# Batch 0 of an attention and gated-MLP kernel: v requested before the second run of q and k, and that run's transposes moved behind the spread of the reciprocals

## The chip, the cores and the metric

One core of a Trainium2 chip. The metric is the device time of one execution in microseconds (us), the median over several executions. Every execution also leaves its span (first to last instruction, some 1.8 us shorter than the time).

## The reference

Sliding-window attention with a linear position bias, then a gated MLP. Cut to what matters:

```python
# q, k, v: (8 batches, 8 heads, 576 positions, 64); window 128
scores = q @ k.T / 8 + bias          # bias: -slope[head] * |i - j|
scores = where(0 <= i - j < 128, scores, -1e9)
attn = softmax(scores)
x = (attn @ v) as (4608 tokens, 512)
out = (gelu(x @ w_gate) * (x @ w_val)) @ w_out    # 512 -> 1536 -> 512
```

The kernel takes exp without subtracting the maximum, multiplies by exp of the bias (a mask that is 0 outside the window), sums, and multiplies the value products by the reciprocals of the sums.

## The kernel before

Everything is scheduled by hand: each engine runs its instructions in program order. Batch 0 is the head of the kernel: nothing can be overlapped with it except its own parts, so its transfers, transposes and exps are interleaved with care. Its positions are handled in two parts: part 0 is positions 0 to 319 (first run of q and k), part 1 is 320 to 575 (second run). All PSUM tiles come from one ring of eight banks, in program order.

The transfers, in order of issue:

```python
load_runs(0, 0, 0, 4)        # first run of q and k, heads 0..3
...
load_runs(0, 0, 4, 8)        # heads 4..7
load_runs(0, 1, 0, 8)        # second run of q and k
load_v(0, (0, 1, 2))         # v, the three tiles that part 0 needs
load_w(0, 256)               # gate and value weights, columns 0..255
load_w(256, 640)
...
```

The helpers that the change moves:

```python
def keep_busy(n): ...        # the next PSUM bank first takes n products of zeros (line 70)

def rest(cs):                # second run: transposes (line 151), two pairs of heads per bank
    for w in (0, 1):         # q, then k
        ps = bank().bitcast(BF16)
        for k, c in enumerate(cs):
            transpose_runs(0, 1, w, c, ps[:, 256 * k:256 * k + 256])
        untangle(act, 0, 1, w, slice(cs[0], cs[-1] + 1), ps)   # ONE copy on ACT (line 165)

def values_first(copies):    # part 0: value products (L358), copied out by ACT and DVE (L377),
    ...                      # spread of the reciprocals (L295), product of the two on DVE (L379)
```

And the head itself:

```python
scores(0, 0, (2, 3))         # scores, exps on ACT (L197), masks on DVE (L200)
scores2(0)
keep_busy(4)
rest((0, 1))
rest((2, 3))
keep_busy(3)
sums0(0)                     # 72 small products (L282), reciprocal on DVE (L286)
values_first((act, dve, act, dve))
scores(0, 1, (0, 1), None, masks)    # part 1: needs the copies of rest; eight exps
scores(0, 1, (2, 3), None, masks)
for f in range(4):
    gate_val(0, f, 0, 320, tails)    # gate and value products of part 0 (L392)
for args in masks:
    mask(*args)
made_last()                  # small memsets on DVE (L482 to L490)
for tail in tails[0:2]: tail()       # gelu on ACT (L398), gated product on DVE (L399)
sums0(1)                     # sums of part 1, second reciprocal
for tail in tails[2:4]: tail()
gate_val(0, 4, 0, 320)
spread4(0, 1, ...)           # second spread (L295)
```

The softmax here doesn't subtract the row's maximum and nothing guards it: scores larger than these inputs give would overflow.

Of the kernel before, what the change touches and what calls it, by code (L numbers as in the profile page):

```python
# [26 lines left out]
def kernel(  # L27
# [39 lines left out]
    def bank():  # L67
        ps = psum.tile([128, 512], FP32, name="ps")
        for _ in range(heat.pop()):
            nc.tensor.matmul(out=ps, lhsT=zeros[:, 0:128], rhs=zeros, start=True, stop=True)  # L70
        heat.append(0)
        return ps

    def keep_busy(n):
        heat[0] = n
# [20 lines left out]
    def load(t, src, b, js=range(5)):  # L96
        for j in js:
            lo = 64 if j == 0 else 0
            nc.gpsimd.dma_start(  # L99
                out=t[lo:128, j, :].rearrange("p (h d) -> p h d", h=H),  # L100
                in_=src[b][:, 128 * j - 64 + lo:128 * j + 64, :].rearrange("h p d -> p h d"))
# [10 lines left out]
    def runs(what, b, n):  # L112
        first, parts, r = RUNS[b][n]
        t, lo, p = (qs, ks)[what][b], 1536 * n, 0
        if (b, n) == (0, 1):

            t, lo = vb[1], 512 + 1024 * what
        elif b == 0:
            p = 64 * what
        return t.rearrange("p j x -> p (j x)")[p:p + parts, lo:lo + 512 * r].rearrange(  # L120
            "p (h x) -> p h x", h=H)

    def load_runs(b, n, h0, h1):
        first, parts, r = RUNS[b][n]
        for what, src in ((0, q), (1, k)):
            nc.gpsimd.dma_start(
                out=runs(what, b, n)[:, h0:h1, :],
                in_=src[b][h0:h1, first:first + parts * r, :].rearrange(
                    "h (p r) d -> p h (r d)", r=r))

    def load_v(b, js=range(5)):
        load(vb[b % 2], v, b, js)

    def load_w(lo, hi):
        for dst, src in ((wg, moe_w_gate), (wv, moe_w_val)):
            nc.gpsimd.dma_start(
                out=dst[:, :, lo:hi],
                in_=src[:, lo:hi].rearrange("(c p) f -> p c f", p=128))
# [5 lines left out]
    def transpose_runs(b, n, what, c, ps):  # L144

        first, parts, r = RUNS[b][n]
        src = runs(what, b, n)
        p = 64 * what if (b, n) == (0, 0) else 0
        for x in range(r):
            for i in (0, 1):  # L150
                nc.tensor.transpose(  # L151
                    out=ps[64 * i:64 * i + 64, parts * x:parts * x + parts],
                    in_=src[:, 2 * c + i, 64 * x:64 * x + 64],
                    identity=ident[p:p + parts, p:p + parts])

    def untangle(copy, b, n, what, c, ps):

        first, parts, r = RUNS[b][n]
        dst = by_pair((qT, kT)[what][b])[:, c, 64 + first:64 + first + parts * r]
        if isinstance(c, int):  # L160
            copy(out=dst.rearrange("p (x r) -> p x r", r=r),  # L161
                 in_=ps[:, 0:parts * r].rearrange("p (r x) -> p x r", r=r))
        else:
            n = c.stop - c.start
            copy(out=dst.rearrange("p c (x r) -> p c x r", r=r),
                 in_=ps[:, 0:n * parts * r].rearrange("p (c r x) -> p c x r", c=n, r=r))
# [22 lines left out]
    def score(b, c, i, j, qj, n, ps, col):  # L189
        nc.tensor.matmul(  # L190
            out=ps[:, col:col + 128 * n].rearrange("p (n t) -> p n t", n=n),
            lhsT=blocks(kT, b, i, c, j, 1).rearrange("p n t -> p (n t)"),
            rhs=blocks(qT, b, i, c, qj, n),
            start=True, stop=True)

    def exp(dst, src):
        nc.scalar.activation(out=dst, in_=src, func=AF.Exp, scale=0.125)  # L197

    def mask(dst, m):
        nc.vector.tensor_tensor(out=dst, in0=dst, in1=m, op=ALU.mult)  # L200

    def scores2(b, later=None):

        P = p2_pool.tile([128, 4, 2, 128], BF16, name="P2")
        probs2[b] = P
        ps = [bank(), bank()]
        for c in range(4):
            for i in (0, 1):
                score(b, c, i, 2, 2, 1, ps[i], 128 * c)
        for i in (0, 1):  # L210
            exp(P[:, :, i, :], ps[i].rearrange("p (c n) -> p c n", c=4))
        if later is None:
            for i in (0, 1):
                mask(P[:, :, i, :], emask[:, i:8:2, 0:128])
        else:
            later.append((P.rearrange("p c i n -> p (c i) n"), emask[:, :, 0:128]))

    def scores(b, s, cs, then=None, later=None):


        pss = []
        for c in cs:
            ps = [bank(), bank()]
            pss.append(ps)
            for j, qj, n, col in (((0, 0, 2, 0), (1, 1, 2, 256)),
                                  ((4, 4, 1, 0), (2, 3, 1, 128), (3, 3, 2, 256)))[s]:
                for i in (0, 1):
                    score(b, c, i, j, qj, n, ps[i], col)
        if then:
            then()  # L230
        for c, ps in zip(cs, pss):
            P = p_pool[s].tile([128, 2, 512], BF16, name="P")
            probs[b, s, c] = P
            for i in (0, 1):
                exp(P[:, i, :], ps[i])
            args = (P.rearrange("p i (n x) -> p i n x", n=2),
                    emask[:, 2 * c:2 * c + 2, :].unsqueeze(2).to_broadcast((128, 2, 2, 256)))
            if later is None:
                mask(*args)
            else:  # L240
                later.append(args)
# [46 lines left out]
    def spread4_banks(b, s):  # L288
        lo, w = PART[s][0], WIDE[s]

        pss = [bank() for _ in range(4)]
        n = (4, 2)[s]
        for k in range(n):
            for g, ps in enumerate(pss):
                nc.tensor.matmul(  # L295
                    out=ps[:, w * k:w * k + w],
                    lhsT=sel[32 * g:32 * g + 32, 2 * k:2 * k + 2, :].rearrange("p i m -> p (i m)"),
                    rhs=row(b)[32 * g:32 * g + 32, lo:lo + w], start=True, stop=True,
                    tile_position=(32 * g, 0))
        return pss  # L300
# [48 lines left out]
    def products(b, s, cs):  # L349
        lo, hi = PART[s]  # L350
        pss = []
        for c in cs:
            ps = bank()
            pss.append(ps)
            for j, a, e in PIECES[s]:
                for i in (0, 1):
                    h = 2 * c + i
                    nc.tensor.matmul(  # L358
                        out=ps[64 * i:64 * i + 64, a:e],
                        lhsT=vb[b % 2][:, j, 64 * h:64 * h + 64],  # L360
                        rhs=prob(b, s, c, i, j, e - a),
                        start=(j == 2 * s), stop=(j == 2 * s + 2), skip_group_check=True)
        return pss
# [8 lines left out]
    def values_first(copies):  # L372


        n, w = PART[0][1], WIDE[0]
        for c, ps in enumerate(products(0, 0, range(4))):
            copies[c](out=recip[0][:, c, 0:n], in_=ps[:, 0:n])  # L377
        for g, ps in enumerate(spread4_banks(0, 0)):
            nc.vector.tensor_tensor(  # L379
                out=xT[:, :, w * g:w * g + w], in0=recip[0][:, :, w * g:w * g + w],  # L380
                in1=ps[:, 0:4 * w].rearrange("p (c x) -> p c x", c=4), op=ALU.mult)
# [68 lines left out]
    for half, base, step, chan in ((0, 0, 1, -1), (1, -1, -1, 1)):  # L450
# [2 lines left out]
            out=t, in_=t, compare_op=ALU.is_ge, fill=1e9,  # L453
            base=base, pattern=[[step, 128]], channel_multiplier=chan)
    load_runs(0, 0, 4, 8)
    load_runs(0, 1, 0, 8)
    load_v(0, (0, 1, 2))
    load_w(0, 256)
    load_w(256, 640)
    load_v(0, (3, 4))  # L460
# [47 lines left out]
    def rest(cs):  # L508
        for w in (0, 1):
# [3 lines that stand above are left out]
            untangle(act, 0, 1, w, slice(cs[0], cs[-1] + 1), ps)  # L513
# [6 lines left out]
    keep_busy(2)  # L520
    scores(0, 0, (2, 3))
    scores2(0)
    keep_busy(4)
    rest((0, 1))
    rest((2, 3))
    keep_busy(3)
    sums0(0)
    masks, tails = [], []
    values_first((act, dve, act, dve))
    scores(0, 1, (0, 1), None, masks)  # L530
    scores(0, 1, (2, 3), None, masks)
    for f in range(4):
# [134 lines left out]
```

## Time and profile before

| | before |
|---|---|
| time, first 3 runs | 358.77 us (358.43 to 359.65) |
| span of the profiled execution | 356.0 us |
| last mask of part 0 ends | 13.02 us |
| sums of part 0 end | 14.47 us |
| eight exps of part 1 start | 17.15 us |
| second spread starts | 25.32 us |

The views are read as follows. The chain that ended last is followed back from the last instruction and gives, for each step, start, length and what ran. A timeline lists instructions in order of time, merged; what stands in brackets at a line's end is the idle time of that engine before it and what ended it. The lines of before are in the prediction below.

### The profile page before, as it was taken

What the parts mean: (1) busy time and instruction counts of PE and PEld (TensorE: products, weight loads), DVE (VectorE), ACT (ScalarE), POOL (GpSimd) and SP (SyncE); (2) the same over time, 40 slices, a digit from 0 to 9 for tenths busy, and PEclk for the clock granted to TensorE, in tenths of its full rate; (3) what the DMA queues carried; (4) which work ended last, traced back from release to release, by engine and by line L of the source; (5) the groups of instructions that cost most, each with busy time, mean ns of one, the idle gap of its engine ahead of it and who ended that gap; (6) DMA issues with size and microseconds to landing.
All of it is one profiled execution on the core that took longest, in us unless ns stands there. A gap on an engine that the chain in (4) does not pass through costs nothing.

```text
span 356.0 us, 7053 instructions
## 1 busy us (share of the span) xinstructions
PE 346.2 (97%) x2823; PEld 174.5 (49%) x2867; DVE 188.6 (53%) x327; ACT 185.8 (52%) x342; POOL 103.3 (29%) x137
## 2 busy tenths in 40 slices
PE   8899999999999999999999999999999999999995
PEld 3568545444454445445454545454444444444443
DVE  4785578344988646656456654755474404403320
ACT  6784495536877375633873297327832233313322
POOL 8853469600930193003900192004000000000000
PEclk9999999999999999999999999999999999999999
DMA  7999999999999299673996499759205020011002
GB/s 91 182 195 197 202 158 199 146 155 162 146 151 175 60 168 194 116 170 45 153 211 149 78 145 203 132 123 98 88 4 133 32 88 1 2 65 53 2 29 88
DMA packets 145632, 42.62 MB, mean 120 GB/s; under 512 B 131608, under 2 KB 138520, under 8 KB 145600
## 3 DMA queue, kind: packets, MB, share of 16 engines
q0 software_dynamic: 106368, 18.88, 69.4%
q1 hardware_dynamic: 36432, 17.31, 22.0%
q10 hardware_dynamic: 2800, 5.99, 7.7%
q8 instruction: 22, 0.36, 0.4%
q14 instruction: 10, 0.08, 0.1%
HBM read 43.65 MB, written 9.53 MB: 149 GB/s over the span
## 4 chain that ended last, share of the span: by engine, by line
PE 88%; DVE 5%; ACT 3%; issue 1%; DMA 1%; DVEq 0%; ACTq 0%; POOLq 0%
PE ps L392 51%; PE ps L415 23%; PE ps L358 5%; PE ps L190 4%; ACT P L197 3%; PE ps L315 2%; DVE P L200 1%; DVE r L321 1%; PE ps L151 1%; PE ps L70 1%; DMA qs<-in_q_dram 1%; PE ps L429 1%; DVE kT L161 1%; PE ps L295 1%; DVE hT L399 0%
## 5 line engine op out<-in xcount | busy, mean ns | idle before, releaser
L399 DVE TENSOR_TENSOR hT<-ps,gelu 128x512 bf16<-128x512 f32 (+2 forms) x115 | 74.3, 653 | 106.4 <-PE ps L392 92.5
L398 ACT ACTIVATE gelu<-ps 128x512 bf16<-128x512 f32 (+2 forms) x115 | 65.1, 571 | 115.5 <-PE ps L392 113.7
L392 PE MATMUL ps<-xT,wv 128*128 128x512 bf16 (+2 forms) x453 | 111.4, 366 | 0.6
L392 PE MATMUL ps<-xT,wg 128*128 128x512 bf16 (+2 forms) x444 | 110.4, 366 | 0.9
L415 PE MATMUL ps<-wo,hT 128*128 128x512 bf16 x402 | 94.6, 380 | 0.8
L197 ACT ACTIVATE P<-ps 128x512 bf16<-128x512 f32 x144 | 73.0, 632 | 8.1 <-PE ps L190 8.0
L392 PEld LDWEIGHTS <-wv 128*128 128x128 bf16 x460 | 44.7, 98 | 48.7
L392 PEld LDWEIGHTS <-wg 128*128 128x128 bf16 x460 | 43.2, 98 | 47.3 <-issue 0.5
L200 DVE TENSOR_TENSOR P<-P,emask 128x1024 bf16<-128x1024 bf16 (+1 forms) x79 | 49.1, 641 | 31.5 <-ACT P L197 31.0
L415 PEld LDWEIGHTS <-hT 128*128 128x128 bf16 x420 | 38.9, 98 | 47.7 <-issue 3.6
L99 POOL DMA_DIRECT2D vb<-in_v_dram x40 | 33.9, 886 | 10.6 <-DMA ks<-in_k_dram 4.3
L420 ACT COPY osb<-ps 128x512 f32<-128x512 f32 x31 | 18.7, 602 | 31.2 <-PE ps L415 30.4
L620 POOL COPY mark<-hT 1x2 bf16<-1x2 bf16 x4 | 0.7, 176 | 98.6 <-DVE hT L399 98.6
L321 DVE RECIPROCAL r<-ps 128x320 f32<-128x320 f32 (+1 forms) x14 | 26.8, 1935 | 1.3 <-PE ps L315 1.3
L99 POOL DMA_DIRECT2D qs<-in_q_dram x30 | 25.2, 857 | 7.2 <-DMA wo<-in_moe_w_out_dram 5.1
L368 DVE TENSOR_TENSOR xT<-ps,rb 128x256 bf16<-128x256 f32 (+1 forms) x60 | 22.9, 445 | 7.2 <-DMA rb<-rd 4.7
L99 POOL DMA_DIRECT2D ks<-in_k_dram x30 | 25.4, 884 | 1.2 <-DMA vb<-in_v_dram 0.7
L190 PE MATMUL ps<-qT,kT 64*128 64x256 bf16 (+1 forms) x384 | 22.1, 244 | 1.6 <-DVE kT L161 0.7
L190 PEld LDWEIGHTS <-kT 64*128 64x128 bf16 x384 | 13.4, 94 | 13.5 <-issue 9.9
L358 PE MATMUL ps<-P,vb 128*64 128x128 bf16 (+2 forms) x384 | 18.3, 244 | 0.1
L358 PEld LDWEIGHTS <-vb 128*64 128x64 bf16 x384 | 14.6, 110 | 5.4 <-issue 4.8
L398 ACT ACT_TABLE_LOAD x7 | 9.0, 1283 | 0.4 <-PE ps L392 0.3
(72 smaller groups left out, 115.2 us busy)
## 6 DMA issues: line engine op xcount, KB each, us to landing
out_dram<-osb SPq DMA_DIRECT2D x35, 256.0 KB, 3.3
rb<-rd ACTq DMA_DIRECT2D x10, 576.0 KB, 7.5
vb<-in_v_dram POOLq DMA_DIRECT2D x32, 128.0 KB, 6.8
qs<-in_q_dram POOLq DMA_DIRECT2D x24, 128.0 KB, 5.9
ks<-in_k_dram POOLq DMA_DIRECT2D x24, 128.0 KB, 6.3
wo<-in_moe_w_out_dram POOLq DMA_DIRECT2D x2, 768.0 KB, 17.5
wg<-in_moe_w_gate_dram POOLq DMA_DIRECT2D x2, 384.0 KB, 9.9
wv<-in_moe_w_val_dram POOLq DMA_DIRECT2D x2, 384.0 KB, 11.0
```

The costliest lines, as they stand in the source:

```text
L99: nc.gpsimd.dma_start(out=t[lo:128, j, :].rearrange("p (h d) -> p h d", h=H), in_=src[b][:, 128 * j - 64 + lo:128 * j + 64, :].rearrange(" ...
L190: nc.tensor.matmul(out=ps[:, col:col + 128 * n].rearrange("p (n t) -> p n t", n=n), lhsT=blocks(kT, b, i, c, j, 1).rearrange("p n t -> p ( ...
L197: nc.scalar.activation(out=dst, in_=src, func=AF.Exp, scale=0.125)
L200: nc.vector.tensor_tensor(out=dst, in0=dst, in1=m, op=ALU.mult)
L321: nc.vector.reciprocal(row(b)[:, lo:hi], ps[:, 0:hi - lo])
L358: nc.tensor.matmul(out=ps[64 * i:64 * i + 64, a:e], lhsT=vb[b % 2][:, j, 64 * h:64 * h + 64], rhs=prob(b, s, c, i, j, e - a), start=(j == ...
L368: nc.vector.tensor_tensor(out=xT[:, c, b * S + lo:b * S + hi], in0=ps[:, 0:hi - lo], in1=recip[b][:, c, lo:hi], op=ALU.mult)
L392: nc.tensor.matmul(out=ps[:, 0:hi - lo], lhsT=w[:, c, 128 * f:128 * (f + 1)], rhs=xT[:, c, t0 + lo:t0 + hi], start=(c == 0), stop=(c == 3))
L398: nc.scalar.activation(out=gl[:, 0:hi - lo], in_=pg[:, 0:hi - lo], func=AF.Gelu)
L399: nc.vector.tensor_tensor(out=hid[g][:, f, lo:hi], in0=pv[:, 0:hi - lo], in1=gl[:, 0:hi - lo], op=ALU.mult)
L415: nc.tensor.matmul(out=po, lhsT=hid[g][:, f, 128 * t:128 * (t + 1)], rhs=wo[:, f, :], start=(f == 0), stop=(f == NF - 1))
L420: (nc.vector.tensor_copy if g < 2 and t < 2 else nc.scalar.copy)(out=osb, in_=po)
```

## The change

The intent, by its own words: v arrives early enough for the value products, the sums follow the masks at once instead of behind transposes and products of zeros, and the second run's transposes move behind the spread, where their data (now later) has landed.

```diff
     load_runs(0, 0, 4, 8)
+    load_v(0, (0, 1, 2))
     load_runs(0, 1, 0, 8)
-    load_v(0, (0, 1, 2))
     load_w(0, 256)
@@
     scores2(0)
-    keep_busy(4)
-    rest((0, 1))
-    rest((2, 3))
-    keep_busy(3)
+    keep_busy(5)
     sums0(0)
     masks, tails = [], []
     values_first((act, dve, act, dve))
+    rest((0, 1))
+    rest((2, 3))
     scores(0, 1, (0, 1), None, masks)
```

## The prediction

> **What bounds the kernel now.** I read the page first, then the chain that ended last in order of time, then the timelines of ACT, DVE and TensorE from 8 to 28 us, then the landing times of the first transfers. From the page, the chain by engine and line:
>
> ```profile
> PE 88%; DVE 5%; ACT 3%; issue 1%; DMA 1%; DVEq 0%; ACTq 0%; POOLq 0%
> PE   8899999999999999999999999999999999999995
> ```
>
> TensorE is 9 tenths busy or more from the third slice on, and the waits of TensorE show no single one over 0.4 us after the start. So behind about 27 us the kernel is a rigid train of matmuls: whatever the first 27 us gain or lose arrives at the end nearly undiminished. The change touches only that head. The chain there (start us, length us, what):
>
> ```profile
> 10.51 0.97 PE ps L70 x4
> 11.48 1.17 PE ps L151 x32
> ...
> 13.02 0.38 PE ps L70
> 13.40 0.74 PE ps L282 x25
> ...
> 14.47 1.26 PE ps L358 x24
> 15.73 1.06 PE ps L295 x32
> 16.79 0.37 PE ps L190 x6
> 17.16 4.02 ACT P L197 x8
> ...
> 21.21 0.69 DVE P L200
> ...
> 23.66 0.74 DVE hT L399 x2
> 24.40 0.88 DVE r L286
> ...
> 25.32 0.73 PE ps L295 x16
> ```
>
> In words: products of zeros (L70), transposes of the second run (L151), zeros again, the sums of batch 0 (L282), the value products (L358), the spread of the reciprocals (L295), the first scores of the second part (L190). Then the chain leaves TensorE: eight exps on ACT in a row (17.16 to 21.18), the last mask on DVE, small memsets on DVE, two gated products, the second reciprocal, and at 25.32 back to TensorE. Between 18.70 and 25.1 TensorE is busy with the first gate and value matmuls, but they do not set the time of the second spread: the exps do. So the number to follow is the start of those eight exps, 17.15 us. ACT and DVE around it (start, length, line, the idle time before in brackets):
>
> ```profile
> 9.52 3.04 ACT L197 ACTIVATE P<-ps 128x512 bf16<-128x512 f32 x6 [0.34 <-PE ps L190]
> 12.40 0.65 ACT L165 COPY qT<-ps 128x512 bf16<-128x512 bf16 x1
> ...
> 13.82 0.70 ACT L165 COPY kT<-ps 128x512 bf16<-128x512 bf16 x1
> ...
> 17.15 4.03 ACT L197 ACTIVATE P<-ps 128x512 bf16<-128x512 f32 x8 [1.20 <-PE ps L190]
> ```
> ```profile
> 9.75 3.27 DVE L200 TENSOR_TENSOR P<-P,emask 128x1024 bf16<-128x1024 bf16 x6
> 14.51 0.66 DVE L286 RECIPROCAL r<-ps 128x80 f32<-128x80 f32 x1 [1.48 <-PE ps L282]
> ```
>
> The masks that the sums need end at 9.75 + 3.27 = 13.02, but the sums end at 14.47: DVE idles 1.48 us before the reciprocal. That is the slack the change goes for. The four copies of the second run's transposes (one each 0.47 us or so, 12.40 to 14.52) lie in ACT time that nobody needs. That is what the change gives away.
>
> **What the Trainium skill says.** "Perfetto Trace Analysis", Tensor Engine Instruction, says ACT and DVE are strict FIFO and only TensorE reorders, and there only weight loads. The trace agrees: ACT runs its copies and exps in program order. So in the changed kernel the eight exps cannot pass the four copies now put right ahead of them. "ScalarE: Activation LUTs", What ACT_TABLE_LOAD costs, gives 186 ns + 0.833 ns per element for an ACTIVATE with immediates and 93 ns of overlap, an estimate of 520 ns pitch at 512 elements; the trace has 4.03 us for eight, 0.50 us each, and I use that. "DMA: Bandwidth & Descriptors", Two DMAs through the same engine are not ordered, says descriptors of one queue start in order, though they need not finish so. The trace agrees in effect: landings follow the order of issue. "TensorE: Matmul & The Clock Gate", Part 1, says an idle window of about 3.4 us halves the clock. The granted clock was 1.00 in every stretch of the first 40 us here, among them 9 to 10 us, where TensorE was busy 0.50 us of 1.00.
>
> **The change part by part.**
>
> 1. The transfers. v (three tiles) moves ahead of the second run of q and k; sizes and count stay. Before, from issue plus landing: q 5.16 + 5.1 = 10.3, k 6.05 + 5.7 = 11.8, v 12.2, 14.0 and 14.7 us.
>
> ```profile
> vb<-in_k_dram POOLq DMA_DIRECT2D x1, 256.0 KB, 5.7
> ```
> ```profile
> vb<-in_v_dram POOLq DMA_DIRECT2D x2, 128.0 KB, 6.3
> 14.74 0.77 PEld L358 LDWEIGHTS <-vb 128*64 128x64 bf16 x20 [0.20 <-DMA vb<-in_v_dram]
> ```
>
> The last v (issued 8.49, landing 6.2 later) was even waited for, 0.20 us. In the changed order v takes the issue slots from 5.16 on. The three v tiles came within 2.9 us of the landing before them, and the first half's last k landed at 4.56 + 3.4 = 8.0, so my estimate is v complete at about 11 to 11.5, well before 13.2 where it is needed. The same bytes then end with k at about 14.7. Everything behind (weights) keeps its place.
>
> 2. The front of the path. Removed ahead of the sums: 32 transposes (1.17 us) and 2 of the 7 products of zeros. Five of these at about 0.24 us (four took 0.97) end at 10.51 + 1.2 = 11.7. From there the sums follow the masks. Those of the first 64 matmuls wait for all but the last mask. After 13.02 remain the last 8 of 72; at 1.07 us for 72 that is 0.12, plus some 0.05 of signalling: sums end at 13.2 instead of 14.47, a gain of 1.27. The value products take 1.06 (1.26 less the 0.20 wait): 14.26. The reciprocal (13.25 + 0.66 = 13.9) is in time for the spread, 1.06 as before: spread ends at 15.33 instead of 16.79, a gain of 1.46. None of the banks used is late: they come from exps that ended by 12.56 and from copies.
>
> 3. The back of the path. Now 32 transposes follow the spread, 15.33 to 16.5. The first eight fill a bank after about 0.33 (before, a group of ten took from 7.83 to 8.15), so ACT starts copying at 15.66. It has been free since the copies of the value products (c0 and c2, done near 14.6). Four copies at the measured pitch of 0.48 (12.40, 12.86, 13.34, 13.82) keep ACT until 15.66 + 1.92 = 17.58. The scores need the second copy (about 16.9), so their first bank is full near 17.3; the exps wait for ACT and not for scores. Exps start at 17.58 against 17.15: a loss of 0.43. In terms of the sum: minus 1.46 on the front, plus 0.33 + 1.92 for transposes and copies, minus the 0.37 of scores that is now covered by the copies = +0.42, about +0.4.
>
> 4. What hangs on it. Exps, last mask, memsets, two gated products and the reciprocal follow without slack on ACT and DVE (4.02 + 0.69 + about 1.8 + 0.74 + 0.88), so the second spread moves from 25.32 to about 25.75. The gate matmuls in between: their banks come from the exps of the first pair (done near 18.6), so they start at about 18.5, like before (18.70), and are done in time. xT for them is ready at about 17.1 rather than 18.55, a gain with no taker. The 0.48 us of zeros saved is TensorE time that turns into idle. After 26 us the same train, 0.4 us later: 358.77 + 0.4 = 359.2 us.
>
> **The rivals.** First: the front's gain reaches the end, because the copies overlap with the scores and the first exps need only the first two. Then 358.77 − 1.4 = about 357.4. For it speaks DVE's idle 1.48 us; against it the program order, which has all four copies ahead of the first exp, and ACT in FIFO order. Second: the moved q and k land late, or wait behind v, and TensorE stands at the transposes. If k landed at 16.5 instead of 14.7, the path would lose about another 1 us: 360.2. Against: the sum of the bytes ahead of it is unchanged, 14.7 stays some 0.9 ahead of need. Third: without zeros in the gaps (my estimates: 0.5 us before 17, 0.4 before 17.9, 0.3 before 13.0) the clock drops for one window; half of 3.4 us lost at most, about 361. Against: no gap is near that window, and as sparse a stretch kept full clock. Fourth: the 0.4 is absorbed, because the second spread has other slack; then 358.8. Against: the chain passes through it.
>
> **Range and chances.** My step lengths are good to some 0.1 us each, with a dozen of them, so ±0.4 on the shift; the three runs before spread from 358.43 to 359.65 themselves. Predicted 359.2, eight in ten between 358.2 and 360.2. Two per cent is 7.2 us, more than everything that lies between 10.5 us and 17.2 us could give or take: within 2% has 0.98; slower by more, through a clock or transfer accident, 0.015; faster 0.005.
>
> **What would show each step.** Right, if in the changed kernel: the sums end at 13.1 to 13.4 and DVE's wait for them shrinks to near 0.2; no wait on v; spread ends near 15.3; ACT's four copies stand at 15.6 to 17.6 directly ahead of the eight exps with no idle time between; the exps start at 17.4 to 17.8; the second spread is at 25.6 to 25.9; behind it the matmul train is the same, shifted. Wrong, if the exps start before 17.15 (then a gain), if TensorE waits on a transfer at the transposes, if the granted clock falls below 1.00 between 12 and 20 us, or if the second spread no longer follows the exps.

## The result

| | runs | median | range |
|---|---|---|---|
| changed | 4 | 358.78 us | 358.52 to 359.07 |
| before | 4 | 358.60 us | 358.37 to 359.65 |

The ratio is 1.000, 95% interval 0.9978 to 1.0021. Ratios here are the mean time of one kernel's fast runs over that of the other's of the same rounds, so not quite the ratio of the medians quoted. The time is the same within 2%, inside the predicted range. No change at all would have been inside it too; whether the small shift of 0.4 us was right needs the profile and more runs.

The chain of the changed kernel in the same stretch, start, length and what:

```profile
10.03 3.20 DVE P L200 x6
...
13.28 0.32 PE ps L282 x6
13.60 1.11 PE ps L358 x24
14.71 1.14 PE ps L295 x32
...
16.64 0.59 ACT kT L165
17.23 0.49 ACT qT L165
17.72 0.49 ACT kT L165
18.21 3.94 ACT P L197 x8
...
25.36 0.88 DVE r L286
...
26.28 0.73 PE ps L295 x16
```

The chain now runs through the masks of DVE, then the sums, and then, where before six scores led from the spread to the exps, through the copies of the transposes on ACT. ACT's timeline has the same without a gap:

```profile
16.16 0.59 ACT L165 COPY qT<-ps 128x512 bf16<-128x512 bf16 x1 [1.23 <-PE ps L151]
...
18.07 4.07 ACT L197 ACTIVATE P<-ps 128x512 bf16<-128x512 f32 x8
```

DVE's masks and first reciprocal:

```profile
9.95 3.27 DVE L200 TENSOR_TENSOR P<-P,emask 128x1024 bf16<-128x1024 bf16 x6
13.63 0.66 DVE L286 RECIPROCAL r<-ps 128x80 f32<-128x80 f32 x1 [0.41 <-PE ps L282]
```

DVE's idle time before the first reciprocal fell from 1.48 to 0.41 us: the front did gain. Yet the exps start at 18.07 instead of 17.15 and the second spread at 26.28 instead of 25.32, 0.96 us later. Far behind it the same group of gate products, before and after:

```profile
64.01 1.03 PE L392 MATMUL ps<-xT,wg 128*128 128x512 bf16 x4
```
```profile
64.97 1.03 PE L392 MATMUL ps<-xT,wg 128*128 128x512 bf16 x4
```

The span is 356.9 instead of 356.0 us. In these two executions nothing of the shift is absorbed.

Not all of the 0.92 us is the change's. The masks of part 0 already start at 9.95 instead of 9.75, and the reason lies ahead of everything that was changed. TensorE's first transposes, before and after:

```profile
4.53 0.50 PE L151 MATMUL ps<-ident,qs 64*64 64x64 bf16 x20 [0.27 <-DMA qs<-in_q_dram]
```
```profile
4.45 0.74 PE L151 MATMUL ps<-ident,qs 64*64 64x64 bf16 x20
```

The same twenty transposes took 0.50 us in one execution and 0.74 in the other, because TensorE came up to full speed somewhat later: the trace's clock record first grants it at 4.01 us before and at 5.23 after. Measured from the start of the masks, the exps stand 8.12 us later in the changed kernel and 7.40 in the one before: 0.72 us is the change's own.

### The profile page after: what moved, and what is told of

Same layout as the page of the kernel before. It is cut to its first block, busy times and chain, and to the rows that moved or that the text cites. A ratio compares the mean times of both kernels' runs of the same rounds, so it can differ in the third digit from the quotient of the medians.

```text
span 356.9 us, 7091 instructions
## 1 busy us (share of the span) xinstructions
PE 348.8 (98%) x2865; PEld 174.5 (49%) x2865; DVE 189.0 (53%) x327; ACT 185.8 (52%) x342; POOL 103.3 (29%) x137
## 3 DMA queue, kind: packets, MB, share of 16 engines
q0 software_dynamic: 106368, 18.88, 69.5%
## 4 chain that ended last, share of the span: by engine, by line
PE 90%; DVE 6%; ACT 2%; DMA 1%; issue 1%; ACTq 0%; DVEq 0%; POOLq 0%
PE ps L392 51%; PE ps L415 25%; PE ps L358 5%; PE ps L190 4%; DVE P L200 2%; PE ps L315 2%; ACT P L197 1%; DVE r L321 1%; DMA qs<-in_q_dram 1%; PE ps L429 1%; PE ps L151 1%; DVE kT L161 1%; PE ps L295 1%; PE ps L70 1%; DVE hT L399 0%
## 5 line engine op out<-in xcount | busy, mean ns | idle before, releaser
L392 PE MATMUL ps<-xT,wg 128*128 128x512 bf16 (+2 forms) x460 | 112.3, 366 | 0.1
L415 PE MATMUL ps<-wo,hT 128*128 128x512 bf16 x420 | 95.8, 380 | 0.0
L99 POOL DMA_DIRECT2D vb<-in_v_dram x40 | 34.0, 889 | 13.1 <-DMA ks<-in_k_dram 5.5
L358 PEld LDWEIGHTS <-vb 128*64 128x64 bf16 x384 | 14.7, 110 | 5.2 <-issue 4.8
```

The source lines that it names most:

```text
L99: nc.gpsimd.dma_start(out=t[lo:128, j, :].rearrange("p (h d) -> p h d", h=H), in_=src[b][:, 128 * j - 64 + lo:128 * j + 64, :].rearrange(" ...
L358: nc.tensor.matmul(out=ps[64 * i:64 * i + 64, a:e], lhsT=vb[b % 2][:, j, 64 * h:64 * h + 64], rhs=prob(b, s, c, i, j, e - a), start=(j == ...
L392: nc.tensor.matmul(out=ps[:, 0:hi - lo], lhsT=w[:, c, 128 * f:128 * (f + 1)], rhs=xT[:, c, t0 + lo:t0 + hi], start=(c == 0), stop=(c == 3))
L415: nc.tensor.matmul(out=po, lhsT=hid[g][:, f, 128 * t:128 * (t + 1)], rhs=wo[:, f, :], start=(f == 0), stop=(f == NF - 1))
```

## The experiments

Twelve runs of nine kernels were made, in four batches, each batch on one chip with its own runs of the kernel before. What the times have in common, first: in every batch some executions, also of the kernel before, are longer than the others by mostly 2 us or a little more. Of the 44 runs of before in the four batches, 33 lie between 357.67 and 358.94 us and 11 between 359.90 and 360.49. Five profiles fell into long executions, all by chance, and all show why. One of them (the last version, second time), first TensorE by time, then the same kernel's row for 4 to 9 us (length, busy time of PE, PEld, DVE, ACT and POOL, then granted clock, DMA share, GB/s):

```profile
9.13 1.04 PE L70 MATMUL ps<-zeros 128*128 128x512 bf16 x2
```
```profile
4.00:9.00 5.00, 4.58 (x53) 2.05 (x53) 2.31 (x6) 2.72 (x9) 5.00 (x7) 1.00 1.09 133
```

Two products of zeros take 1.04 us at 9.13 us; in the profile of before, at 4.96 us, the same two take 0.61. The row prints a granted clock of 1.00 all the same, but this is the view's doing: the trace's clock record has no entry before full speed is first granted, and the view counts a stretch without an entry as full. The first entry stands at 9.24 to 10.62 us in these five profiles and at 3.94 to 5.23 us in the others (6.13 in that of experiment 3), and the masks of part 0 start at 11.9 to 12.4 us instead of 9.8 to 10.1 (10.4 in experiment 3). I call them late starts. For the runs without a profile this is inferred from the time alone. Where it matters, I give medians without the runs that are longer by this gap and say so.

**1. The changed kernel again.**

> The changed kernel as it is, again, in five rounds. Both profiles so far differ by 0.92 us at the start of the eight exps, by 0.96 at the second spread and by 0.9 in the span, while the medians of the timed runs differ by only 0.2. Theory A (the shift of the head reaches the end, part of it is chance between two executions): 0.4 to 0.9 us slower than before, exps at 17.9 to 18.2 us. Theory B (it is absorbed later): within 0.2 us of before although the exps stand late again.

Six runs: five of 358.58 to 358.77 and one of 361.37. Ratio to before 1.0021 (0.9992 to 1.0051). Without the long run of either kernel (one of 6, one of 11) the medians are 358.69 and 358.1: 0.6 us slower. The profile has the masks at 9.85, the exps at 17.96, 8.11 us behind them, and the second spread at 26.18. This agrees with theory A, and not with B. The interval of the ratio includes 1, so the time alone does not prove a loss; the two profiles, equal to 0.01 us from masks to exps, show that the shift of the exps repeats. In this second profile v was complete only at 13.1 us and k at 15.8, so the transfers were nearly late, though no instruction waits for them.

**2. The order alone: transposes moved, transfers as before.**

```diff
     load_runs(0, 0, 4, 8)
-    load_v(0, (0, 1, 2))
     load_runs(0, 1, 0, 8)
+    load_v(0, (0, 1, 2))
```

> The new order of the matmuls, but v again behind the second run of q and k. If v must be early for the new order, the value products wait for the last v at about 14.7 us instead of starting at 13.5, the exps start near 19.1 and the span is about 1.0 us over the changed kernel's. If v's place did not matter, the exps stay at 18.1.

Ratio 1.0061 (1.0038 to 1.0084), six runs from 359.81 to 361.68. The three shorter ones have a median of 359.98, 1.3 us above the changed kernel's 358.69. The profile fell into a late start, where v had landed when it was wanted (exps at 20.42), so it was taken again:

> The new order with v behind, again, for a profile: the first profile fell into an execution in which TensorE ran its first products at half speed until 9.4 us, so that v had landed when it was wanted. In an execution that is fast from 4.5 us on I expect a wait of about 1.0 us on v within the value products and the exps near 19.1; in a slow one, no wait and the exps near 20.4.

```profile
14.19 1.40 PE L358 MATMUL ps<-P,vb 128*64 128x256 bf16 x22 [0.27 <-DMA vb<-in_v_dram]
```
```profile
14.59 0.77 PEld L358 LDWEIGHTS <-vb 128*64 128x64 bf16 x20 [0.30 <-DMA vb<-in_v_dram]
18.95 4.07 ACT L197 ACTIVATE P<-ps 128x512 bf16<-128x512 f32 x8
```

This execution ran at full speed from about 5.3 us. The value products wait for v and the exps start at 18.95, as expected (near 19.1), 0.9 us later than in the changed kernel. So the new order needs v early.

**3. The transfers alone: the order as before, v ahead.**

```diff
     load_runs(0, 0, 4, 8)
-    load_runs(0, 1, 0, 8)
     load_v(0, (0, 1, 2))
+    load_runs(0, 1, 0, 8)
```

> The order of the matmuls of before, with v requested ahead of the second run of q and k. If the two parts of the change need each other, the transposes of k stand ahead of the sums and wait for k, which then lands at 15.2 to 15.7 us instead of 11.8; 24 transposes, the zeros, sums, products, spread and scores follow, so the exps start near 20.9 and the time rises by 3.5 to 4 us. If TensorE's clock also drops in the wait of nearly 4 us (the rival of the prediction on the clock), matmuls behind it take twice as long for a while and the time rises by 5 us or more. If v's place alone brought something, the time would not rise.

Ratio 1.0103 (1.0077 to 1.0130), runs 361.39 to 362.59. The transposes wait for q and for k, and then the clock falls; TensorE by time, and then two stretches of time, columns as above (granted clock is the third figure from the end):

```profile
13.93 0.41 PE L151 MATMUL ps<-ident,vb 128*64 128x128 bf16 x8 [1.79 <-DMA vb<-in_q_dram]
15.42 0.86 PE L151 MATMUL ps<-ident,vb 128*64 128x128 bf16 x24 [1.08 <-DMA vb<-in_k_dram]
```
```profile
16.00:18.00 2.00, 1.78 (x49) 0.90 (x47) 0.00 (x0) 1.44 (x3) 1.14 (x2) 0.59 1.33 203
18.00:20.00 2.00, 2.00 (x66) 1.83 (x58) 0.66 (x1) 0.28 (x1) 0.74 (x1) 0.55 1.38 198
```

Both halves of the change are losses by themselves, and they belong together. By the ratio the rise is 3.7 us, by the medians (362.3 against 358.08 for before without its two long runs) 4.2, where I expected 3.5 to 4 from the waits and 5 or more with a fall of the clock. The clock did fall: the profile has the exps at 21.96, 4.8 us later than before, of which 0.7 is a later start of the masks. So the fall cost less than I had set for it. The trace's record has the clock at one half from 16.37 to 19.79 us; the two rows above are means over that. It also gives the prediction's third rival its due: such a fall exists, and here it came after more idle time than the changed kernel has. In the 3.41 us before 16.37 TensorE was busy 1.36 us; in the changed kernel's stretch of that length with the gaps behind the spread, 15.47 to 18.88 us, it was busy 2.54 and the clock stayed full.

**4. Half of the copies back under the masks ("split").** The helpers `load_runs` and `rest` take one more argument for this, which of q and k to handle; that part of the diff is left out.

```diff
     load_runs(0, 0, 4, 8)
+    load_runs(0, 1, 0, 8, (0,))     # q of the second run
     load_v(0, (0, 1, 2))
-    load_runs(0, 1, 0, 8)
+    load_runs(0, 1, 0, 8, (1,))     # k of the second run
@@
-    keep_busy(5)
+    keep_busy(2)
+    rest((0, 1), (0,))              # transposes of q
+    rest((2, 3), (0,))
+    keep_busy(2)
     sums0(0)
@@
     values_first((act, dve, act, dve))
-    rest((0, 1))
-    rest((2, 3))
+    rest((0, 1), (1,))              # transposes of k
+    rest((2, 3), (1,))
```

> The changed kernel with q's half of the second run back in the wait for the masks: q's transfer stands before v, k's behind, q's transposes ahead of the sums, k's behind the spread; two of the four ACT copies lie again before 13.6 us. If the four copies ahead of the exps are what costs, the exps start 0.9 to 1.0 us earlier than in the changed kernel (17.0 to 17.3), and the span is 0.7 to 1.0 lower. If late transposes or the transfers cost, and not the copies, little of it comes back: the exps at 17.7 or later.

```profile
12.60 1.14 ACT L165 COPY qT<-ps 128x512 bf16<-128x512 bf16 x2
...
16.16 1.07 ACT L165 COPY kT<-ps 128x512 bf16<-128x512 bf16 x2 [1.23 <-PE ps L151]
17.23 4.03 ACT L197 ACTIVATE P<-ps 128x512 bf16<-128x512 f32 x8
```

The first copy behind the spread starts at 16.16 us, exactly as in the changed kernel; only two of the four copies have gone from there, and the exps start 0.84 us earlier. The time: ratio to before 1.0010 (0.9976 to 1.0044), with two long runs of six; the other four have a median of 357.86, 0.8 us below the changed kernel's 358.69 of the same batch. This is the test of the main step: the copies on ACT ahead of the exps are what holds the exps: two copies at the measured pitch of 0.48 us are 0.96, the exps came 0.84 us earlier, and the time without long runs fell by 0.8. The transposes do not hold them: both copies and the exps follow each other on ACT without a gap. (One of the two long runs, 361.49, is longer by 3.6 us, which is more than a late start explains.)

**5. The memsets early, in the changed kernel.**

```diff
+    made_last()
     for args in masks:
         mask(*args)
     masks.clear()
-    made_last()
```

> The changed kernel with the small memsets of DVE moved ahead of the second part's masks, into the 1.7 us in which DVE then waits for the exps. If the chain exps, last mask, memsets, gated products, reciprocal sets the second spread, this takes the 1.76 us of memsets out of it until the next wait: the first gelu ends at about 23.9, sums end at 24.75, reciprocal at 25.7, so the second spread moves from 26.28 to 25.7 to 25.85 and the span falls by 0.4 to 0.6. If TensorE or ACT alone set the second spread, nothing moves.

Ratio 1.0025 (0.9997 to 1.0052); without two long runs the median is 358.68, no better than the changed kernel's 358.69. So the expected 0.4 to 0.6 us did not come. The profile was in a late start; again:

> The changed kernel with early memsets, again, for a profile in an execution fast from 4.5 us on. The timed runs of the first were no faster than the changed kernel. If the landing of the second weight transfer is the reason, as in the two other kernels with early memsets, the third value product waits for it until about 22 us and the second spread stands at 25.9 to 26.1, behind TensorE and not behind DVE.

```profile
22.11 1.28 ACT L398
...
23.40 0.45 ACT gelu L398
...
23.89 0.88 PE ps L282 x32
24.76 1.19 PE ps L392 x8
25.96 0.69 PE ps L295 x16
```

The one timed run was 358.35. The second spread comes at 25.92, where I expected it (25.9 to 26.1), but not for the reason I gave. The weights landed at 21.5 and hardly held anything. From the last exp the chain now runs over ACT's table load (1.28 us) and the first gelu, which frees the bank that the second sums wait for, and then over TensorE. From exps to second spread it is 7.90 us against 8.21 in the changed kernel: the memsets' 1.76 us shrink to 0.31, since ACT's table load stands beside them. That 0.31 us is not resolved by the timed runs.

**6. The kernel before without its three products of zeros.**

```diff
     rest((2, 3))
-    keep_busy(3)
     sums0(0)
```

> The kernel before without the three products of zeros ahead of the sums. If the zeros are paid time (what the change's wording suggests), everything behind them comes 0.75 us earlier and so does the end. If they only fill a wait, the sums end 0.7 us earlier but the value products still wait for the last v at 14.7 us, the exps start at 17.0 to 17.2 as before, and the time stays within 0.2 us.

Ratio 0.9999 (0.9971 to 1.0028). Without two long runs the median is 357.93, against 358.08 for before (nine runs): within the 0.2 us of a filled wait, and not 0.75. The profile is of a late start and cannot show the wait on v. It has another stop instead:

```profile
14.60 0.80 PE ps L282 x26
15.40 1.35 issue
16.74 0.27 PE ps L282 x4
```

For 1.35 us, in the middle of the sums, TensorE waits for nothing that the profile shows; the last mask ended at 15.13 and all of v had landed by about 14.5. Both profiles of the last version (experiment 8) stop as well, within the value products, for 0.17 and 0.34 us, and all three stops end at 16.72 to 16.74 us and behind 447 to 449 recorded matmuls and weight loads. All three are late starts; in the five late profiles the first fetch in the queue that the page calls "instruction" begins at 14.2 to 14.5 us, in the others at 10.0 to 11.9. So a wait of TensorE for its own instructions is likely, but no run tests it.

**7. The kernel before with the memsets early** (the diff of experiment 5).

> The kernel before with DVE's small memsets ahead of the second part's masks. If only DVE's chain sets the second spread there, it gains over 0.5 us. By the timelines TensorE follows closely behind (sums end at 24.0, one gate and value product to 25.1), so I expect the second spread at 25.0 to 25.1 instead of 25.3 and 0.2 to 0.3 us less in all.

Ratio 1.0011 (0.9985 to 1.0038), three of six runs long. The second spread stayed at 25.32, where I expected 25.0 to 25.1. The chain says why:

```profile
11.61 9.94 DMA wv<-in_moe_w_val_dram
...
21.59 1.80 PE ps L392 x12
23.40 0.80 PE ps L282 x32
24.20 1.19 PE ps L392 x8
25.39 0.69 PE ps L295 x16
```

With DVE out of the way, the landing of the second weight transfer at 21.55 us takes its place: a wait hidden just behind the one removed.

**8. Split and early memsets, and then smaller weights.**

> Both at once: q's half of the second run under the masks, k's behind the spread, and the memsets early. In the profile of the split alone the second spread stands at 25.40, behind DVE's reciprocal, and one value product waits 0.63 us for its weights (to 21.4). If the weights do not bind, the second spread comes to 25.0 to 25.1, 0.3 us less than the split alone; if the weights land at 22 us or later in this execution, nothing is gained.

Ratio 0.9990 (0.9964 to 1.0017); without the one long run the median is 357.62, against 358.08 for before. The second spread is at 25.42 and its chain too starts at the weights' landing, at 21.61: the second case of the expectation (a bind by the landing), a little earlier than I had set it. So the last step cuts that transfer:

```diff
-    load_w(256, 640)
+    load_w(256, 512)
+    load_w(512, 640)
```

> The split with early memsets, and the second weight transfer (columns 256 to 640) cut in two (256 to 512, 512 to 640). In the profiles with early memsets the chain runs through the landing of that transfer's second matrix at 21.5 to 21.6 us, and the second spread stands at 25.4. If the landing is what now binds, the first piece lands before 20.9, the wait of 0.64 us in the third value product goes, and the second spread comes to 24.9 to 25.0: 0.4 to 0.5 us less than split_memset, about 357.2. If something else binds, the spread stays at 25.4.

> The last version again, since its profile fell into an execution with TensorE at half speed until 10.2 us, where no weight was waited for anyway. In an execution fast from 4.5 us on: no wait in the third value product, and the second spread at 24.9 to 25.1 if the landing of the second weight transfer was what bound split_memset (25.42), or still at 25.4 if not. Its runs of that kind near 357.4 against 358.1 of before.

The first time three of six runs, and six of eleven of before, were long: ratio 0.9986 (0.9950 to 1.0021). The second time: ratio 0.9968 (0.9944 to 0.9992), 357.31 to 357.82 in six runs and two long ones, against 357.71 to 358.94 in nine of before and two long ones. This is the only version whose interval against before lies below 1: some 0.3%, or 0.2% (0.75 us) by the medians without the long runs (357.54 and 358.29). Both profiles fell into late starts, where no weights are waited for in any version, so that the second spread moved to 25.0 is not shown. They do show the first piece of the weights landing at 20.82 and 19.83 us instead of 21.61; otherwise only the time speaks for it. The ratio needs care: 0.9968 is what five runs of this kernel, none of them long, give against ten of before, two of them long. Without those two the means give 0.998.

## Why the prediction was right

The time, 358.78 us against 359.2 predicted (358.2 to 360.2), within 2%, was right. Part of that is luck. The shift of 0.4 us was added to 358.77, the median of three runs, but worked out from the profile of an execution that took 357.76; without long runs the kernel before stood at 358.1 to 358.4 in the four batches. So the base was some 0.4 to 0.7 us too high and the shift 0.2 to 0.3 too small, and the two errors partly cancel. One reading was wrong: "the granted clock was 1.00 in every stretch of the first 40 us" holds only from 4.01 us on, where the clock record begins; the seven first products of zeros took 3.05 us, some 0.44 each, against 0.24 later. By its own steps:

1. **The transfers.** v complete at about 11 to 11.5: in the profile after it landed at 11.2 (issued 6.7, landing 4.5 later), and no instruction waits for it. k at about 14.7: it landed at 8.5 + 6.7 = 15.2, half a microsecond later than I estimated, with 0.5 us in hand. The order-only run shows what this step is worth.

2. **The front.** The sums were to end at 13.2 and ended at 13.60, or 13.40 less the late speed-up. This is the term that was mis-sized. I gave the last 8 products 0.12 us for issue and 0.05 for signalling. But the last of them also needs its own time from issue to result: the profile has 0.32 us from the first product behind the last mask to the end (13.28 to 13.60). "TensorE: Matmul & The Clock Gate" in the Trainium skill, Single matmul latency, gives (398 + N)/2.4 ns for a product that fills the array. For 80 columns that is an estimate of 0.20 us (these products use 32 of the array's columns); with the 0.12 for issue it makes the 0.32 measured. The line of before that would have told me stood in its chain, six products in 0.32 us. Value products and spread took 1.11 and 1.14 us instead of 1.06 each. In all the front gained 0.33 us less than I worked out.

3. **The back.** First copy 0.31 us behind the spread (predicted 0.33), four copies in 1.91 us (1.92), exps directly behind them. The split confirmed that these copies, and not the transposes or the transfers, hold the exps.

4. **The sum and the end.** Predicted +0.42 us at the exps, measured +0.72 us net of the start; the second spread and the whole train behind it followed the exps, to the last 0.1 us of the span. In the timed runs it is 0.6 us without late starts. The direction and the mechanism were right, the size 0.3 us short, by the front's terms. The places that the prediction gave as signs were missed for that: the exps stand at 18.07 (17.4 to 17.8 expected) and the second spread at 26.28 (25.6 to 25.9), and without the 0.20 of the late speed-up still at 17.87 and 26.08.

**The rivals.** The first (the front's gain arrives) is refuted: the exps start later, directly behind the four copies on ACT. The second (late landing) did not occur in the changed kernel, though its second profile came close, and did in the transfers-only one. The third (the clock) did not occur behind the moved work; in the transfers-only run, it did. The fourth (absorption) is refuted in the profiles by the train 0.96 us later at 65 us; the timed runs alone do not decide it. What none of the rivals saw is the other clock effect: late starts move single runs by 2 us, three times the change.

## What to carry to other kernels

When work is moved out of a wait, look at every engine that it uses, not only at the one that waits: here TensorE's transposes were free to move, but their copies went from idle ACT time to the place directly ahead of the exps that set the chain. Splitting the moved work by when its data arrives (q early, k late) took the loss back (0.84 us at the exps), but alone it was no faster than the kernel before (ratio 1.0010). And when two bounds lie within half a microsecond, taking one away shows the next, so each removal needs its own profile and runs sorted by how they started.

## What the Trainium skill lacked or had wrong

- "TensorE: Matmul & The Clock Gate", Part 1, lets the moment of full speed vary by ±500 ns from run to run (and elsewhere warns that the count of slow products varies). Here the clock record first grants it at 3.9 to 5.2 us (once 6.1) or at 9.2 to 10.6 us with the same seven products of zeros at the start, and a late one costs some 1.8 to 2.7 us of time (358.1 against 359.9 to 360.5 in the kernel before, 357.5 against 360.2 in the last version), 0.5% or more of this kernel. The record's complete entries last 3.413, 10.24, 341.33, 348.16 or 351.57 us, that is 1, 3, 100, 102 or 103 times 3.413, which fits the page's free-running window. Why full speed comes only at a later step in some executions was not tested.
- The same page's rule (HAM oscillation) is no idle gap over about 3.4 us. In the transfers-only run two gaps of 1.79 and 1.08 us with eight transposes between them were enough: TensorE was busy 1.36 of the 3.41 us to 16.37 us, and then the clock was at one half until 19.79. The page does say elsewhere that frequent short idling makes the clock swing, but not how much of it.
- "ScalarE: Activation LUTs", What ACT_TABLE_LOAD costs: the estimate of 520 ns pitch for 512 elements is 500 ns here (4.03 us for eight). Its 1.28 us for a table load agrees; the stall of about 1.38 us it adds for the drain is not seen, the first gelu starts 0.01 us behind the load.
